# Square passes timed by the attention's row maxima, and three PSUM banks that are handed out oldest first

## The chip, the cores and the metric

One core of one Trainium2 chip runs the whole program in one launch. The metric is the device time of that launch in microseconds (us), lower being better. TensorE (PE) multiplies, VectorE (DVE), ScalarE (ACT) and GpSimd (POOL) do the rest, and SyncE (SP) issues nearly all transfers. Each engine works through its own queue in order; an instruction that must wait for another engine holds up everything behind it on its own queue. PSUM, into which TensorE writes, has eight banks here, each 128 partitions by 512 float32.

## The reference

For 8 batches: banded causal attention (8 heads, 576 positions, head size 64, a window of 128 and a slope per head), the real part of a two-dimensional Fourier transform added to its output, a layer norm, and a feed-forward network of width 2048 with a residual.

```python
scores = scale * np.matmul(q, k.transpose(0, 1, 3, 2))
...
scores = np.where(mask, scores + bias[None], -1000000000.0)
scores = scores - np.max(scores, axis=-1, keepdims=True)
attn = np.exp(scores)
attn = attn / (np.sum(attn, axis=-1, keepdims=True) + 1e-09)
return np.matmul(attn, v).astype(np.float32)
...
X = np.fft.fft(x, axis=1)
X = np.fft.fft(X, axis=2)
u = x + np.real(X)
un = (u - mu) / np.sqrt(var + 1e-06)
ch = np.maximum(un @ w_ch1, 0.0) @ w_ch2
return (u + ch).astype(np.float32)
```

## The kernel before

**Work.** The 8 batches have 4 pairs of heads each, so there are 32 pairs p, with b = p // 4. A pair's attention is three groups of scores (`scores`, L387): TensorE writes them into the PSUM tiles `sp0` and `sp1`, VectorE adds the bias and takes each row's maximum in one instruction per tile (L415, into the small tile `nb`), and ScalarE takes the exponential with `nb` as its bias (shown at L169, the helper `after`). From batch 2 on (NF = 2) products run on fp16 pairs: ScalarE rounds to the high half (L428), VectorE makes the low half (shown at L169), SP transposes both by DMA (L437, `pt<-P`), and `values` (L453) multiplies with v into `pv`; `weigh` (L479) divides by the row sums into X (L491). Batches 0 and 1 work in float32 and transpose on TensorE instead (`turn`, L439); there `warm` (L321) adds products that nobody reads, a number of them behind each turn.

When a batch's heads are done, `fourier` (L522) folds X on VectorE, multiplies it by tables on TensorE (`rows`, `middle`, `cols`) and adds the result to X; `norm` (L695) normalizes and sends it through DMA transposes to `uT`. The feed-forward `ffn` (L737) multiplies `uT` by the first weights in steps (L752: 24 matmuls of 256 columns fill one PSUM tile `fp`), ScalarE takes the ReLU (L757), VectorE makes the low half `hbuf` (L169), and the second product (L767: 48 matmuls of 512 columns fill one `fp`) is added to X by VectorE (`X<-fp`, or `ut<-fp` for the rest rows that two batches share) and stored.

**Scale passes.** For each batch from 2 on, `batch_scales` (L258) needs a bound of the sums of squares of q, k and v: 15 chunks are fetched by DMA into slots of `wall` (L273) and squared by ScalarE with a running sum into `mx` (L278, the "Square"). From batch 3 on (75 chunks) each fetch is held back: POOL first copies one element into the slot (L272), from the piece of X that `weigh` was last recorded to write (`last[-1]`), and the DMA has to follow that copy. `top` (L282) and `total` (L152) finish a pass.

**Order.** Every step is put on a heap with a due time in units of about 5 us, and the kernel's main loop records them in order of these times (`put`, `after`); the constants at the top are due times and lengths of steps. A scheduler of the language then orders each engine's queue by its own model of time and by the data dependencies that it sees, so a small copy that depends on other work also moves what follows it.

**Banks.** Four of the eight hold `sp0` and `sp1`, one `pv`. Two more form the pool `ps_f`, used in turn for `fp` (feed-forward; in batch 0 some of the transform). The last, `ps_d` (tile `pd`), holds the sums of the scale passes and the transform's products from batch 1 on, one after another.

Of the kernel before, what the change touches and what calls it, by code (L numbers as in the profile page):

```python
# [22 lines left out]
NF = 2  # L23
# [21 lines left out]
E0 = 18.423  # L45
W1A, N0 = 1.058, 20
WL = (-2.569, 0.042)
PL, VL = 8.86, 2.996
FL, SA, SD, SB, SE = 1.9, 16.181, 0.696, 24.163, 1.152
DFT = 29.394  # L50
START = 48.432
PACE, T1 = (0.447, 0.427), 13.742
SPIN, GAP = 5, 0.73
SLOW = 1.609
W2A, W2D, W2B, W2E = 13.895, 0.631, 21.285, 0.429
W1D, W1B, W1E = 0.379, 11.116, 0.508
F0 = 6.021
SW = 184
SPIN1 = 1


def begin_of(p):
    return 6 * PACE[0] * p if p < 4 else T1 + 6 * (p - 4)


def transform_of(b):
    return T1 + 24 * (b - 1) + DFT if b else PACE[0] * DFT

# [14 lines left out]
def attn_fft_ffn_kernel(  # L83
# [24 lines left out]
    ps_f, ps_s = pool("ps_f", 2, space=PSUM), pool("ps_s", 2, space=PSUM)  # L108
    ps_v, ps_d = pool("ps_v", 1, space=PSUM), pool("ps_d", 1, space=PSUM)
# [42 lines left out]
    def total(m):  # L152
        sums = ps_d.tile([128, 512], F32, name="pd")[:, 0:m.shape[1]]
        T.matmul(sums, misc[:, 7:8].broadcast_to([128, 128]), m, start=True, stop=True)
        return sums
# [20 lines left out]
    last = []  # L176

    def weights(wi, t0, dt, t1, dt1):
# [26 lines left out]
        def gram(c):  # L205
            if c == 0:
                box["gram"] = ps_f.tile([128, 512], F32, name="fp")[:, 0:128]
# [50 lines left out]
    def batch_scales(b, t0, dt):  # L258
# [6 lines left out]
        def fetch(x, fl, o, n):  # L265
# [5 lines left out]
            if b > NF:  # L271
                G.tensor_copy(box[x][1][0:1, 0:1], last[-1])  # L272
            nc.sync.dma_start(out=box[x][1], in_=fl[:, o:o + n])  # L273

        def part(x, i, c):
            slot, t = box.pop(x)
            held.discard(slot)
            A.activation(t, t, AF.Square, accum_out=box["mx"][:, i, c:c + 1])  # L278

        def top():  # L280
            m1 = small.tile([128, 3], F32, name="m1")
            V.tensor_reduce(m1, box["mx"], AX.X, ALU.max)  # L282
            box["sums"] = total(m1)

        def scale():
            r = small.tile([128, 3], F32, name="r")
            root_inv(r, box["sums"])
            sc = small.tile([128, 8], F32, name="sc", bufs=3)
# [98 lines left out]
    def scores(p, i):  # L387
# [19 lines left out]
        for e in range(2):  # L407
# [3 lines left out]
            for ti in grp:  # L411
# [4 lines left out]
                                       mul, 3.0e38, ALU.add, ALU.min, nb[:m, ti:ti + 1])  # L416
                after(0.25, A.activation, pt[:m, 0:n], pt[:m, 0:n], AF.Exp, bias=nb[:m, ti:ti + 1], scale=-1.0)
# [21 lines left out]
    def turn(p, i, e):  # L439
# [11 lines left out]
        after(GAP, warm, upper, SPIN if p < 4 else SPIN1)  # L451
# [27 lines left out]
    def weigh(p, e, pv):  # L479
# [13 lines left out]
        last.append(Xs[b][0:1, 0, h * D:h * D + 1])  # L493
# [441 lines left out]
```

## Time and profile before

| | us |
|---|---|
| median of 3 runs (1077.57 to 1080.9) | 1079.5 |
| the profiled execution, its own time | 1086.17 |
| its span (first to last instruction) | 1083.9 |
| TensorE busy in the span | 1039.0 |
| VectorE, ScalarE, POOL busy | 703.2, 583.0, 48.0 |
| granted clock, mean | 0.984 |

The 2.3 us between the span and the execution's own time lie outside the instructions. A row of a wait view names who waited, whose end released it, the total, how often, and the longest. In the timeline a bracket gives the engine's idle time before the row and what ended it. TensorE's matmuls overlap in their pipeline, so a row of one matmul is longer than the distance to the next.

### The profile page before, as it was taken

What the parts mean: (1) busy time and instruction counts of PE and PEld (TensorE: products, weight loads), DVE (VectorE), ACT (ScalarE), POOL (GpSimd) and SP (SyncE); (2) the same over time, 40 slices, a digit from 0 to 9 for tenths busy, and PEclk for the clock granted to TensorE, in tenths of its full rate; (3) what the DMA queues carried; (4) which work ended last, traced back from release to release, by engine and by line L of the source; (5) the groups of instructions that cost most, each with busy time, mean ns of one, the idle gap of its engine ahead of it and who ended that gap; (6) DMA issues with size and microseconds to landing.
All of it is one profiled execution on the core that took longest, in us unless ns stands there. A gap on an engine that the chain in (4) does not pass through costs nothing.

```text
span 1083.9 us, 23935 instructions
## 1 busy us (share of the span) xinstructions
PE 1039.0 (96%) x9208; PEld 726.4 (67%) x9208; DVE 703.2 (65%) x2073; ACT 583.0 (54%) x1388; POOL 48.0 (4%) x136
## 2 busy tenths in 40 slices
PE   8998889899899999999899999999999999999998
PEld 5876776675667667675657667584757676757655
DVE  4889789687674868687674858678784836252111
ACT  6886987558444567567554556556544522241000
POOL 0000001000000000001100000001000000000000
PEclk8998989999999999999999999999999999999999
DMA  9961466727542364527643364537522330030000
GB/s 365 346 218 56 123 147 158 151 54 187 136 101 75 97 147 123 147 51 152 170 109 74 96 146 119 143 54 134 110 60 34 53 69 11 10 60 11 20 10 21
DMA packets 191506, 117.81 MB, mean 109 GB/s; under 512 B 154400, under 2 KB 164128, under 8 KB 191392
## 3 DMA queue, kind: packets, MB, share of 16 engines
q1 hardware_dynamic: 190816, 114.84, 42.4%
q8 instruction: 72, 1.18, 0.5%
q10 hardware_dynamic: 576, 1.45, 0.3%
q14 instruction: 42, 0.34, 0.1%
HBM read 70.63 MB, written 9.44 MB: 74 GB/s over the span
## 4 chain that ended last, share of the span: by engine, by line
PE 61%; DVE 16%; DMA 9%; ACT 7%; issue 3%; SPq 2%; POOL 1%; ACTq 0%; DVEq 0%; POOLq 0%
PE fp L752 25%; PE fp L767 22%; PE sp L403 4%; DMA wall<-v_dram 4%; DVE P L415 2%; DMA wall<-q_dram 2%; ACT wall L278 2%; PE pd L602 2%; PE pv L468 2%; DVE P L169 1%; PE pd L636 1%; DVE hbuf L169 1%; DMA pt<-P 1%; ACT P L169 1%; PE sp L446 1%
## 5 line engine op out<-in xcount | busy, mean ns | idle before, releaser
L767 PE MATMUL fp<-wall,hbuf 128*128 128x512 f16 x1728 | 391.2, 379 | 0.0
L752 PEld LDWEIGHTS <-wall 128*128 128x128 f16 x3840 | 338.5, 99 | 70.4 <-issue 25.2
L752 PE MATMUL fp<-uT,wall 128*128 128x256 f16 x3072 | 365.4, 275 | 20.2 <-DVE hbuf L169 11.9
L767 PEld LDWEIGHTS <-hbuf 128*128 128x128 f16 x1728 | 162.8, 98 | 184.9 <-issue 3.5
L757 ACT ACTIVATE hbuf<-fp 128x512 f16<-128x512 f32 x144 | 84.8, 589 | 202.0 <-PE fp L752 201.9
L169 ACT ACTIVATE P<-P,nb 128x256 f32<-128x256 f32 x320 | 141.9, 477 | 60.8 <-DVE nb L415 60.5
L169 DVE SCALAR_TENSOR_TENSOR hbuf<-fp,hbuf 128x512 f16<-128x512 f32 x144 | 98.8, 686 | 99.3 <-ACT hbuf L757 98.4
L169 DVE SCALAR_TENSOR_TENSOR P<-P 128x256 f16<-128x256 f32 x240 | 87.4, 391 | 40.4 <-ACT P L428 38.9
L415 DVE CUSTOM_DVE_ANT_0 P<-sp,rg,nsl 128x256 f32<-128x256 f32 x240 | 97.5, 449 | 13.7 <-PE sp L403 12.0
L278 ACT ACTIVATE wall<-wall 128x512 f32<-128x512 f32 (+2 forms) x90 | 54.4, 605 | 91.3 <-DMA wall<-k_dram 33.5
L403 PE MATMUL sp<-kk,qq 64*128 64x256 f16 (+5 forms) x880 | 95.0, 287 | 1.4 <-ACT pt L449 0.7
L428 ACT ACTIVATE P<-P 128x256 f16<-128x256 f32 x240 | 84.1, 382 | 2.4 <-DMA pt<-P 1.7
L473 PE MATMUL pv<-vhs,pt 128*128 128x65 f16 x432 | 56.0, 195 | 1.2 <-DMA pt<-P 1.1
L474 PE MATMUL pv<-vl,pt 128*128 128x64 f16 x432 | 55.9, 193 | 0.0
L169 DVE SCALAR_TENSOR_TENSOR X<-fp,misc,X 128x512 f32<-128x512 f32 x32 | 23.8, 744 | 48.4 <-PE fp L767 48.3
L475 PE MATMUL pv<-vhs,pt 128*128 128x65 f16 x432 | 55.1, 194 | 0.0
L403 PEld LDWEIGHTS <-qq 64*128 64x128 f16 (+1 forms) x720 | 32.4, 99 | 24.6 <-issue 18.8
L473 PEld LDWEIGHTS <-pt 128*128 128x128 f16 x432 | 41.0, 98 | 9.6 <-issue 1.3
L752 PE MATMUL fp<-wall,wall 128*128 128x128 f16 x768 | 46.2, 219 | 0.0
L474 PEld LDWEIGHTS <-pt 128*128 128x128 f16 x432 | 40.7, 99 | 6.1
L468 PEld LDWEIGHTS pv<-vr,pt 128*128 128x128 f32 x288 | 37.6, 199 | 6.1 <-PE pv L323 3.3
L272 POOL COPY wall<-X 1x1 f32<-1x1 f32 x75 | 26.2, 377 | 343.9 <-DVE X L491 265.0
(159 smaller groups left out, 1205.9 us busy)
## 6 DMA issues: line engine op xcount, KB each, us to landing
qr<-q_dram SPq DMA_DIRECT2D x32, 304.0 KB, 3.2
hbuf<-w_dram SPq DMA_DIRECT2D x16, 512.0 KB, 7.7
out_dram<-X SPq DMA_DIRECT2D x32, 256.0 KB, 2.2
wall<-v_dram SPq DMA_DIRECT2D x30, 256.0 KB, 3.5
vr<-v_dram SPq DMA_DIRECT2D x24, 320.0 KB, 4.1
kr<-k_dram SPq DMA_DIRECT2D x24, 289.0 KB, 3.8
wall<-q_dram SPq DMA_DIRECT2D x24, 256.0 KB, 3.0
wall<-k_dram SPq DMA_DIRECT2D x24, 256.0 KB, 3.1
```

The costliest lines, as they stand in the source:

```text
L169: put(now[0] + dt, lambda: f(*a, **kw))
L278: A.activation(t, t, AF.Square, accum_out=box["mx"][:, i, c:c + 1])
L403: T.matmul(sp[e][:m, col:col + n], qq[h, c0:c0 + m], keys(kk[h], ti), start=(x == 0), stop=(x == len(prods) - 1))
L415: V.tensor_tensor_reduce(pt[:m, 0:n], sp[e][:m, col:col + n], tab[:m, pc:pc + n], mul, 3.0e38, ALU.add, ALU.min, nb[:m, ti:ti + 1])
L428: A.activation(hi, P32, AF.Copy, scale=2.0 ** 14)
L468: T.matmul(pv[:, ti], pt[:, col:col + 128], ops[p][2][:, e, vc], start=first, stop=last)
L473: T.matmul(pv[:, ti], ph, vh[:, e, vc], start=first, stop=False)
L474: T.matmul(pv[:, ti, 0:D], ph, vl[:, e, vc], start=False, stop=False)
L475: T.matmul(pv[:, ti], pl, vh[:, e, vc], start=False, stop=last)
L752: T.matmul(fp[:, i * n:(i + 1) * n], w1_ap(e, c, f0 + i), uT[:, j, c, 0:n], start=(c == 0 and p == 0), stop=(c == 3 and p == 2))
L757: A.activation(ht[:, 0], fp, AF.Relu)
L767: T.matmul(op, hh[f][:, a, i * 128:(i + 1) * 128], w2_ap(e, f), start=(f == 0 and p == 0), stop=(f == 15 and p == 2))
```

## The change

Three things are edited. First, the POOL copy ahead of a fetch reads `mark[-1]`, the row maximum last recorded, where it read the last piece of X; and a new POOL instruction ahead of each of these 75 Squares writes zero (a row maximum minus itself) into the cell of `mx` that the Square then fills, so that the Square follows the row maximum last recorded at its own due time. Second, three banks are now one set: up to the start of the feed-forward of batch 1 they are given out as before, and from then on `take` gives the one that was given back the longest ago (`give`, recorded with the last reader). Third, due times change: among them the distance of the pairs of batch 1 (0.911 of a unit's six), the start of the feed-forwards, the length of a transform (1.386 for 1.609), the lead of a fetch (2.073 for 1.9), and six `warm` products in place of five behind each turn of pair 1.

```diff
-FL, SA, SD, SB, SE = 1.9, 16.181, 0.696, 24.163, 1.152
+FL, SA, SD, SB, SE = 2.073, 16.745, 0.696, 24.163, 1.152
-SLOW = 1.609
-W2A, W2D, W2B, W2E = 13.895, 0.631, 21.285, 0.429
+SLOW = 1.386
+W2A, W2D, W2B, W2E = 16.635, 0.564, 21.18, 0.402
...
-    return 6 * PACE[0] * p if p < 4 else T1 + 6 * (p - 4)
+    return 6 * PACE[0] * p if p < 4 else T1 + 6 * PQ * (p - 4) if p < 8 else T1 + T2 + 6 * (p - 4)
...
-    ps_f, ps_s = pool("ps_f", 2, space=PSUM), pool("ps_s", 2, space=PSUM)
-    ps_v, ps_d = pool("ps_v", 1, space=PSUM), pool("ps_d", 1, space=PSUM)
+    ps_s, ps_v = pool("ps_s", 2, space=PSUM), pool("ps_v", 1, space=PSUM)
+    banks = [pool(f"ps_b{i}", 1, space=PSUM) for i in range(3)]
+    stamp, taken, late, turn2, ticks = [0, 0, 0], {}, [], cycle((0, 1)), count(1)
+
+    def take(key, name):
+        assert key not in taken
+        if late:
+            i = min((i for i in range(3) if i not in taken.values()), key=lambda i: stamp[i])
+        else:
+            i = next(turn2) if name == "fp" else 2
+        taken[key] = i
+        return banks[i].tile([128, 512], F32, name=name, tag="bank")
+
+    def give(key):
+        stamp[taken.pop(key)] = next(ticks)
...
             if b > NF:
-                G.tensor_copy(box[x][1][0:1, 0:1], last[-1])
+                G.tensor_copy(box[x][1][0:1, 0:1], mark[-1])
             nc.sync.dma_start(out=box[x][1], in_=fl[:, o:o + n])
...
             held.discard(slot)
+            if b > NF:
+                G.tensor_tensor(box["mx"][0:1, i, c:c + 1], mark[-1], mark[-1], ALU.subtract)
             A.activation(t, t, AF.Square, accum_out=box["mx"][:, i, c:c + 1])
...
+                mark.append(nb[0:1, ti:ti + 1])
                 after(0.25, A.activation, pt[:m, 0:n], pt[:m, 0:n], AF.Exp, bias=nb[:m, ti:ti + 1], scale=-1.0)
...
-        last.append(Xs[b][0:1, 0, h * D:h * D + 1])
...
+    def lower(key, ht, fp):
+        V.scalar_tensor_tensor(ht[:, 1], fp, 0.0, ht[:, 0], ALU.max, ALU.subtract)
+        give(key)
+
+    def joined(key, t, op):
+        V.scalar_tensor_tensor(t, op, wone, t, ALU.mult, ALU.add)
+        give(key)
+
     def ffn(b):
+        if b:
+            late.append(b)
...
-                fp = ps_f.tile([128, 512], F32, name="fp")
+                key = ("first", b, slot, f0)
+                fp = take(key, "fp")
```

How the order moves is shown at the fifth chunk of q of batch 4 (384 wide). On POOL, where `X` is the output of batch 3 and `nb` a group's row maxima, the fetches of batch 4's first six chunks stood before like this (the fifth chunk's copy is in the fourth row):

```order
L272 COPY wall0_109<-X_2498 1x1 x2
L272 COPY wall1_110<-X_2498 1x1
L642 MEMSET ab_2771 128x2
L272 COPY wall0_109<-X_2498 1x1 x2
L272 COPY wall1_110<-X_2498 1x1
L263 MEMSET mx_5464 128x15
```

and after the change, from the second chunk on, like this (the fifth chunk's copy is the first that reads `nb_3836`, and its Square's own instruction is in the last row):

```order
L732 TENSOR_TENSOR rstd_3032<-rstd_3032,misc_97 128x2
L288 COPY wall0_112<-nb_3600 1x1
L288 COPY wall1_113<-nb_3600 1x1
L295 TENSOR_TENSOR mx_3560<-nb_3600 1x1
L732 TENSOR_TENSOR rstd_3130<-rstd_3130,misc_97 128x1
L288 COPY wall0_112<-nb_3701 1x1
L295 TENSOR_TENSOR mx_3560<-nb_3701 1x1
L288 COPY wall0_112<-nb_3836 1x1
L295 TENSOR_TENSOR mx_3560<-nb_3836 1x1 x2
L288 COPY wall1_113<-nb_3836 1x1
L288 COPY wall0_112<-nb_3988 1x1
L295 TENSOR_TENSOR mx_3560<-nb_3988 1x1 x2
```

The fetches no longer stand in bunches behind one piece of X, but one or two to a group of row maxima. On ACT, the same chunk's Square (`mx`, 384 wide) stood before among these (L169 with `nb` is an exponential, L757 a ReLU):

```order
L169 ACTIVATE P_3999<-P_3999,nb_3998 128x256
L757 ACTIVATE hbuf_108<-fp_3794 128x512
L378 ACTIVATE qq_4245<-qr_4084,nsl_3346 128x608
L428 ACTIVATE P_4033<-P_3999 128x256
L378 ACTIVATE kk_4325<-kr_4085,sc_3340 128x578
L169 ACTIVATE P_4002<-P_4002,nb_4001 128x256
L428 ACTIVATE P_4035<-P_4002 128x256
L278 ACTIVATE wall0_109,mx_3542<-wall0_109 128x384
L757 ACTIVATE hbuf_108<-fp_3857 128x512
L278 ACTIVATE wall1_110,mx_3542<-wall1_110 128x512
L278 ACTIVATE wall0_109,mx_3542<-wall0_109 128x512
L757 ACTIVATE hbuf_108<-fp_3915 128x512
```

and after the change among these:

```order
L448 ACTIVATE P_3866<-P_3834 96x256
L183 ACTIVATE P_3839<-P_3839,nb_3836 96x256
L296 ACTIVATE wall1_113,mx_3560<-wall1_113 128x512
L448 ACTIVATE P_3868<-P_3837 128x256
L296 ACTIVATE wall0_112,mx_3560<-wall0_112 128x512
L448 ACTIVATE P_3870<-P_3839 96x256
L788 ACTIVATE hbuf_111<-fp_3873 128x512
L788 ACTIVATE hbuf_111<-fp_3921 128x512
L397 ACTIVATE qq_4260<-qr_4073,nsl_3356 128x608
L183 ACTIVATE P_3986<-P_3986,nb_3985 128x256
L183 ACTIVATE P_3989<-P_3989,nb_3988 128x256
L296 ACTIVATE wall0_112,mx_3560<-wall0_112 128x384
```

Where two exponentials of the group ahead (`nb_3998`, `nb_4001`) stood between older work and the Square, there are now the end of the group whose maximum let the fetch go (`nb_3836`) and all of the next one (`nb_3985`, `nb_3988`). On DVE, the piece of X that released the fetch (L491, `X_2498`) stood before between the row maxima `nb_3998` and `nb_4001`, the latter being what the last exponential ahead of the Square reads:

```order
L415 ISA P_3999,nb_3998<-sp0_3990,rg_3349,nsl_3346 128x256
L415 ISA nb_3998 128x1
L169 SCALAR_TENSOR_TENSOR P_3882<-P_3851,P_3882 128x256
L169 SCALAR_TENSOR_TENSOR hbuf_108<-fp_3763,hbuf_108 128x512
L169 SCALAR_TENSOR_TENSOR P_3884<-P_3853,P_3884 96x256
L489 TENSOR_SCALAR ri_3814<-pv_3656,sc_1997 128x5
L490 RECIPROCAL ri_3814<-ri_3814 128x5
L491 TENSOR_TENSOR X_2498<-pv_3656,ri_3814 128x5x64
L415 ISA P_4002,nb_4001<-sp1_3991,rg_3349,nsl_3346 128x256
L415 ISA nb_4001 128x1
L169 SCALAR_TENSOR_TENSOR hbuf_108<-fp_3794,hbuf_108 128x512
L169 SCALAR_TENSOR_TENSOR qq_4245<-qr_4084,nsl_3346,qq_4245 128x608
```

After the change the fetch goes with `nb_3836` (first row), and the last exponential ahead of the Square reads `nb_3988`:

```order
L434 ISA P_3839,nb_3836<-sp1_3818,rg_3359,nsl_3356 96x256
L434 ISA nb_3836 96x1
L183 SCALAR_TENSOR_TENSOR P_3864<-P_3832,P_3864 128x256
L758 SCALAR_TENSOR_TENSOR hbuf_111<-fp_3804,hbuf_111 128x512
L183 SCALAR_TENSOR_TENSOR P_3866<-P_3834,P_3866 96x256
L183 SCALAR_TENSOR_TENSOR P_3868<-P_3837,P_3868 128x256
L183 SCALAR_TENSOR_TENSOR P_3870<-P_3839,P_3870 96x256
L758 SCALAR_TENSOR_TENSOR hbuf_111<-fp_3873,hbuf_111 128x512
L758 SCALAR_TENSOR_TENSOR hbuf_111<-fp_3921,hbuf_111 128x512
L434 ISA P_3986,nb_3985<-sp0_3977,rg_3359,nsl_3356 128x256
L434 ISA nb_3985 128x1
L434 ISA P_3989,nb_3988<-sp1_3978,rg_3359,nsl_3356 128x256
```

Before, one row maximum lay between the release of the fetch and the last exponential ahead of the Square; now seven rows of other work and a whole next group do.

## Rows read from the trace of the kernel before

**Rows 1.** The page's first part, busy time, share of the span and number of instructions of each engine.

```profile
PE 1039.0 (96%) x9208; PEld 726.4 (67%) x9208; DVE 703.2 (65%) x2073; ACT 583.0 (54%) x1388; POOL 48.0 (4%) x136
```

**Rows 2.** The windows view of five stretches: length, busy time and number of instructions of TensorE, its weight loads, VectorE, ScalarE and POOL, then the granted clock, the DMA engines' share and GB/s. Scale passes run in the first four stretches, none in the last.

```profile
66.00:165.00 99.00, 88.28 (x676) 70.53 (x674) 82.69 (x257) 83.04 (x185) 2.68 (x12) 0.90 0.47 127
165.00:284.00 119.00, 109.23 (x1006) 74.39 (x1005) 90.99 (x277) 78.18 (x197) 9.71 (x24) 0.99 0.62 141
284.00:529.00 245.00, 235.95 (x2235) 162.15 (x2234) 170.88 (x516) 142.21 (x354) 15.01 (x43) 1.00 0.48 115
529.00:773.00 244.00, 237.58 (x2241) 163.01 (x2239) 175.50 (x525) 139.54 (x344) 15.23 (x34) 0.99 0.48 112
773.00:895.00 122.00, 122.00 (x1176) 83.97 (x1175) 77.64 (x218) 52.50 (x126) 1.69 (x5) 1.00 0.32 60
```

**Rows 3.** The waits view of TensorE between 165 and 773 us: who waited for whom, total us, times, longest.

```profile
PE fp L752 <- DVE hbuf L169: 11.9, 10, 2.7
PE fp L752 <- DVE X L169: 4.3, 3, 2.3
PE fp L752 <- DVE ut L169: 3.5, 2, 2.5
PE pd L602 <- DVE zl L610: 3.5, 3, 2.1
PE pv L473 <- DMA pt<-P: 1.1, 1, 1.1
PE pd L602 <- ACT fh L575: 0.8, 1, 0.8
```

**Rows 4.** The waits view of ScalarE over the whole span, its waits for the fetches of the scale passes.

```profile
ACT wall L278 <- DMA wall<-k_dram: 33.5, 17, 4.6
ACT wall L278 <- DMA wall<-q_dram: 29.0, 14, 5.1
ACT wall L278 <- DMA wall<-v_dram: 28.5, 13, 5.2
```

**Rows 5.** The timeline of 272.9 to 281 us, the rows of several engines in order of time: start, length, engine, line, what, in brackets the idle time before it and what ended it.

```profile
272.97 0.49 DVE L491 TENSOR_TENSOR X<-pv,ri 128x320 f32<-128x320 f32 x1
273.59 0.41 POOL L272 COPY wall<-X 1x1 f32<-1x1 f32 x3 [18.05 <-ACT P L428]
274.99 0.52 SPq L273 DMA_DIRECT2D wall<-q_dram  x1
277.96 0.19 PE L475 MATMUL pv<-vhs,pt 128*128 128x65 f16 x1
277.99 0.19 PE L473 MATMUL pv<-vhs,pt 128*128 128x65 f16 x1
278.98 0.52 ACT L278 ACTIVATE wall<-wall 128x384 f32<-128x384 f32 x1 [3.88 <-DMA wall<-q_dram]
279.51 0.58 ACT L757 ACTIVATE hbuf<-fp 128x512 f16<-128x512 f32 x1
280.11 0.69 DVE L169 SCALAR_TENSOR_TENSOR hbuf<-fp,hbuf 128x512 f16<-128x512 f32 x1 [3.49 <-ACT hbuf L757]
280.86 0.38 PE L752 MATMUL fp<-uT,wall 128*128 128x256 f16 x2 [2.67 <-DVE hbuf L169]
```

**Rows 6.** The source view of L272, POOL's copies ahead of the fetches: duration in ns as least, median and longest, first and last start; below it what they waited for (us, times).

```profile
L272 POOL COPY wall<-X x75: 173/174/2801, 140.0 to 693.9; 1x1 f32<-1x1 f32 x75
  DVE X L491: 265.0, 24
```

**Rows 7.** The source view of L273, the fetches: time from issue to landing, in us.

```profile
DMA to landing us min/median/max: 2.1/3.2/6.1
```

**Rows 8.** The timeline around 757 us, rows of VectorE and TensorE.

```profile
756.61 0.06 DVE L544 MEMSET pm<- 96x4 f32 x1 [3.59 <-DMA uT<-un]
758.77 0.74 DVE L169 SCALAR_TENSOR_TENSOR X<-fp,misc,X 128x512 f32<-128x512 f32 x1
759.57 0.60 PE L752 MATMUL fp<-uT,wall 128*128 128x256 f16 x4 [2.31 <-DVE X L169]
```

**Rows 9.** The windows view of two stretches of 4 us, columns as in rows 2.

```profile
281.00:285.00 4.00, 4.00 (x27) 2.98 (x26) 0.69 (x1) 0.79 (x3) 0.00 (x0) 0.57 0.69 146
646.00:650.00 4.00, 3.93 (x21) 2.90 (x21) 1.24 (x4) 0.57 (x2) 0.00 (x0) 0.57 0.68 169
```

**Rows 10.** The chain of waits in order of time, two of its last pieces: start, length, what.

```profile
954.99 20.72 PE fp L767 x96
975.71 20.96 PE fp L752 x192
```

**Rows 11.** The page's fifth part, groups of instructions: busy us, mean ns of one, idle before. A ReLU and its low half, an exponential.

```profile
L757 ACT ACTIVATE hbuf<-fp 128x512 f16<-128x512 f32 x144 | 84.8, 589 | 202.0 <-PE fp L752 201.9
L169 DVE SCALAR_TENSOR_TENSOR hbuf<-fp,hbuf 128x512 f16<-128x512 f32 x144 | 98.8, 686 | 99.3 <-ACT hbuf L757 98.4
L169 ACT ACTIVATE P<-P,nb 128x256 f32<-128x256 f32 x320 | 141.9, 477 | 60.8 <-DVE nb L415 60.5
```

**Rows 12.** The waits view of TensorE from 0 to 165 us, its two longest entries.

```profile
PE pv L323 <- ACT pt L449: 3.1, 2, 2.2
PE pv L323 <- DVE X L491: 2.8, 1, 2.8
```

**Rows 13.** The groups of TensorE by line, the products that nobody reads.

```profile
L323 PE MATMUL pv<-pt 128*128 128x184 bf16 x144 | 20.9, 253 | 5.9 <-ACT pt L449 3.1 <-DVE X L491 2.8
```

More of the change, by code (lines that the diff above doesn't have):

```diff
@@ L150, in view, with total @@
         return bass.AP(tensor=t.tensor, offset=t.offset + off, ap=[t.ap[0]] + [list(d) for d in dims])
-    def total(m):
-        sums = ps_d.tile([128, 512], F32, name="pd")[:, 0:m.shape[1]]
+    def total(key, m):
+        sums = take(key, "pd")[:, 0:m.shape[1]]
         T.matmul(sums, misc[:, 7:8].broadcast_to([128, 128]), m, start=True, stop=True)
@@ L175, in attn_fft_ffn_kernel @@
     weighed, valued = [0] * B, [0] * 4 * B
-    last = []
+    mark = []
     def weights(wi, t0, dt, t1, dt1):
@@ L206, in gram @@
             if c == 0:
-                box["gram"] = ps_f.tile([128, 512], F32, name="fp")[:, 0:128]
+                box["gram"] = take(("gram", wi), "fp")[:, 0:128]
             upper = words(c)[1].bitcast(BF16).rearrange("p (x e) -> p x e", e=2)[:, :, 1]
@@ L282, in top @@
             V.tensor_reduce(m1, box["mx"], AX.X, ALU.max)
-            box["sums"] = total(m1)
+            box["sums"] = total(("scale", b), m1)
         def scale():
@@ L287, in scale @@
             root_inv(r, box["sums"])
+            give(("scale", b))
             sc = small.tile([128, 8], F32, name="sc", bufs=3)
@@ L450, in turn @@
         upper = pt.bitcast(BF16).rearrange("p (x e) -> p x e", e=2)[:, :, 1]
-        after(GAP, warm, upper, SPIN if p < 4 else SPIN1)
+        after(GAP, warm, upper, SPL[p])
     def values(p, i, e):
@@ L512, in attn_fft_ffn_kernel, with bank @@
     uts, uTs = {}, {}
-    spare = cycle((ps_f, ps_d, ps_f))
-    def bank(b):
-        if b == 0:
-            p = next(spare)
-            return p.tile([128, 512], F32, name="fp" if p is ps_f else "pd")
-        return ps_d.tile([128, 512], F32, name="pd")
+    spare = cycle(("fp", "pd", "fp"))
+    def bank(key):
+        return take(key, next(spare) if key[1] == 0 else "pd")
     def fourier(b, t0):
@@ L594, in rows @@
         def rows(g):
-            zp = st["zp", g] = bank(b)
+            zp = st["zp", g] = bank(("rows", b, g))
             o = 0 if g < 2 else 2
@@ L610, in rows_lo @@
             V.scalar_tensor_tensor(zl, st["zp", g][:, :NS], 2.0 ** -19, st["zh", g], ALU.mult, ALU.subtract)
+            give(("rows", b, g))
         def middle():
-            gps = st["gps"] = bank(b)
+            gps = st["gps"] = bank(("middle", b))
             for j, (j0, mj) in enumerate(SCH):
@@ L625, in middle_out @@
                 A.activation(gt[:mj, 1, j:j + 1], gt[:mj, 0, j:j + 1], AF.Copy, scale=-1.0)
+            give(("middle", b))
         gw = (129, 128, 128, 127)
@@ L631, in cols @@
             j0, m = SCH[j]
-            mp = st["mp", j] = bank(b)
+            mp = st["mp", j] = bank(("cols", b, j))
             for g in range(4):
@@ L665, in cols_add @@
                 V.tensor_tensor(ut[p0 + 64:p0 + 96], X2[64:96], ds[64:96, 0:512], ALU.add)
-        f = (SLOW if b > 1 else 0.9) if b else PACE[1]
+        f = (SLOW if b > 1 else F1) if b else PACE[1]
         put(t0, begin)
@@ L757, in ffn @@
                 A.activation(ht[:, 0], fp, AF.Relu)
-                after(0.2, V.scalar_tensor_tensor, ht[:, 1], fp, 0.0, ht[:, 0], ALU.max, ALU.subtract)
+                after(0.2, lower, key, ht, fp)
                 for i in range(per):
@@ L762, in ffn @@
             for i, t in enumerate(tiles):
-                op = ps_f.tile([128, 512], F32, name="fp")
+                key = ("second", b, slot, i)
+                op = take(key, "fp")
                 for f in range(16):
@@ L770, in ffn @@
                         yield
-                after(0.15, V.scalar_tensor_tensor, t, op, wone, t, ALU.mult, ALU.add)
+                after(0.15, joined, key, t, op)
                 after(0.4, nc.sync.dma_start, out=ov[slot + i], in_=t)
@@ L777, in attn_fft_ffn_kernel @@
         b, j = divmod(p, 4)
-        t, f = begin_of(p), 1 if b else PACE[0]
+        t, f = begin_of(p), 1 if b > 1 else (PACE[0], PQ)[b]
         lead = t - (7 if b else PL) * f if p else -3.2
```

29 lines of the change are left out of this document (17 added, 12 removed).

## Prediction

> **What bounds the kernel now.** I read the page's busy shares first, then the stretches, then who waits for whom, and last the timeline at one wait. TensorE is busy 1039.0 of 1083.9 us [rows 1], so at most some 45 us of its idle time can be won, and the rest of the time is matmuls that the change leaves as they are. The stretches say where that idle time lies [rows 2]: 10.7 us in 66 to 165, 9.8 in 165 to 284, 9.1 in 284 to 529, 6.4 in 529 to 773, and nothing in 773 to 895. The last stretch still has attention, a transform and feed-forward side by side, but no scale pass. That is the best control in this trace: without the passes, two banks for the feed-forward and one for the transform let TensorE run without a gap.
>
> Between 165 and 773 us, 25.1 us of waits have names [rows 3]. In nearly all, TensorE wants a bank and VectorE has not read it yet. VectorE is not the cause: ScalarE waits 91.0 us in all, 44 times, at a Square whose chunk has not landed [rows 4], and the ReLUs behind it wait too. At 273 us the whole chain can be seen [rows 5]: weigh writes X at 272.97, POOL copies three times in a bunch at 273.59, the fetch is issued at 274.99, the Square starts at 278.98 after 3.88 us of idle, the ReLU follows at 279.51, VectorE reads the bank at 280.11, and TensorE, idle for 2.67 us, goes on at 280.86. X written to Square started took 6.0 us. In the order before, only one row maximum stands on VectorE between that X and the last exponential ahead of this Square.
>
> **The Squares' waits.** I counted over both orders how many VectorE instructions lie between the one that releases a fetch (or what POOL and SP must pass before it) and the one that the last ScalarE instruction ahead of its Square needs. Before, the median of the 75 held-back chunks is 3, and for 32 it is zero or less; after the change it is 23, and none is zero or less. A VectorE record lasts 703.2 / 2073 = 0.34 us, and VectorE is busy 65% of the time, so 23 are some 8 to 12 us, an estimate, against the 6.0 us that the chain needs (of which 3.2 us median landing [rows 7]). Some 12 instructions, 4 us of work or 6 with idle, are then the border; counting to 15 to be safe, 70 of 75 lie under it before and 15 of 73 after (for two, other waits hide the fetch). So I keep 20% of what the waits cost and let 80% go.
>
> What they cost TensorE: the waits for `hbuf` (11.9), `ut` (3.5), `zl` (3.5) and `fh` (0.8) [rows 3], 19.7 us. 80% of it is 15.8. Bounds: 0, if something else is late next, and 19.7.
>
> **The banks.** A bank of the feed-forward's first product holds 24 matmuls of 20.96 / 192 = 0.109 us, 2.6 us; one of the second holds 48 of 20.72 / 96 = 0.216 us, 10.4 us [rows 10]. Emptying a bank takes a ReLU of 0.59 and a low half of 0.69 us [rows 11]. With two banks, the second `fp` of a batch takes the bank of the last second product, one block of 2.6 us after that ended. At 757 us VectorE stood 3.59 us for a DMA transpose that was still reading its buffer, so the addition to X came at 758.77 and TensorE waited 2.31 us [rows 8]. Oldest first, that block takes a bank that was freed before or during that second product; in the order, 11 to 15 us of matmuls lie between its last use and this one for batches 2 to 5. The three `X` waits (4.3 us) should go by the same 80%: 3.4. Where the transform runs, it now shares the three banks with the feed-forward. Its own reuse comes no sooner (3.1 us of matmuls at the tightest for `rows` before, and after once the set is shared), but the single tile of `middle` and the one after it have only 2.7 to 3 us where they had up to 5.4. One feed-forward block of batch 1 has 1.6 us behind `middle`; I charge 1 us for these. The first transform from the old single bank, batch 1's, stays as tight as it was.
>
> **What each wait costs on top.** A matmul's record is 0.19 us where the next could start 0.03 us later [rows 5], so a wait of the list is some 0.16 us longer than printed: 80% of 20 waits, 16 x 0.16 = 2.6. And behind two of the longest the granted clock is 0.57, from 281 to 285 and from 646 to 650 us [rows 9], that is the lower of its two levels, 1.2 GHz, for most of it and 2.4 GHz for the rest: 2 x 4 x 0.43 = 3.4 us. With the waits gone I let this go too.
>
> **What is added.** 75 POOL instructions of one element, 0.17 us median each if they last as the copies do [rows 6]. They wait for the same row maximum as an exponential that ScalarE has to run ahead of the Square anyway, 0.48 us [rows 11], which covers 0.17; uncovered, they would be 75 x 0.17 = 12.8 us of ScalarE, of which TensorE felt 19.7 / 91.0 = 0.22, so 2.8 us. The row maxima's buffer is used again only some 50 VectorE instructions later. Here a page speaks against the change: the Trainium skill, "SBUF — State Buffer", section "Who interferes with whom", says that a VectorE instruction with two SBUF inputs and a GpSimd instruction that reads SBUF exclude each other for a whole instruction. The longest copy, 2.8 us against a median of 0.17, would fit that, the median does not. By the row's median the sum has nothing for this; by the rule at its worst it would be turned into a loss of some 15 us, which is rival 4.
>
> **Due times and the start.** Six more dummy products are 0.25 us at most each by their record, 20.9 / 144 = 0.15 by busy time [rows 13]: 6 x 0.15 = 0.9. Up to 165 us the order moves everywhere, with waits of 3.1 and 2.8 us at the dummy products [rows 12]; there ScalarE and VectorE are busy 83 of 99 us beside TensorE's 88 [rows 2], so nothing is free. The banks are as before there. In the order, batch 0's feed-forward is some 3 us further when batch 2's scores begin, and other waits are tighter. I take 0, with 6 us either way.
>
> **Sum.** 15.8 + 3.4 + 2.6 + 3.4 - 1 - 0.9 = 23.3. The profiled execution took 1086.2 us, 2.3 of it outside its span, so 1062.9 there; it ran 6.7 us above the median, and I take that to be the same part of a later run. From the median, 1079.5 - 23.3 = 1056.2.
>
> **Rivals.** (1) Something else is late next. VectorE is busy 76% of 165 to 284 [rows 2], and its queue of low halves can be the limit when ScalarE no longer is; half of the sum comes, 1068. Against it stands the last stretch without a gap, with VectorE at 64%. (2) All of it goes, with no wait left as in the last stretch: 25.1 + 3.2 + 3.4 = 31.7, less 1.9, and some 3 us in the start: 1047. (3) The start loses 6 to 8 us by the new due times, and the rest comes as summed: 1063. (4) Slower: the new POOL instruction heads the way of each Square. If VectorE's work holds it up, it lasts up to the 2.8 us of the longest copy [rows 6]; less the 0.48 us that an exponential covers, 75 x 2.3 = 173 us of ScalarE, times 0.22 is 38 us more, against 23 won: 1094. It decides from about 1.9 us each on ((23.3 / 0.22) / 75 = 1.4, plus 0.48); the 75 copies show a median of 0.17, so it is unlikely. (5) The pacing does not bind, because landings stretch as far as releases move ahead: the time stays, 1079.
>
> **How the numbers follow.** Forecast 0.5, rival 1 0.17, rival 2 0.16, rival 3 0.10, rival 4 0.04, rival 5 0.03. The likeliest time is 1056. The range 1045 to 1068 takes in the forecast with its start either way, rival 2's time, rival 3 and the upper half of rival 1. About 0.3% (3.2 us) is what a measurement can tell from no change; faster than that: 0.92, within: 0.04, slower: 0.04.
>
> **What would show it.** Right: ScalarE's waits for the fetches fall from 91.0 to 30 us or less; TensorE's waits for `hbuf`, `ut` and `zl` after 165 us fall under 6 us; no lower clock after 165 us; POOL's copies no longer come in threes. Wrong: Squares that now wait for POOL, row maxima that wait for it, or more idle time of TensorE in 66 to 165 us than 10.7 us.

## The result, and the profile after

| | median us | against before, 95% interval |
|---|---|---|
| before, run beside it | 1080.2 (4 runs) | |
| after | 1052.77 (4 runs, 1049.97 to 1052.84) | 0.9736 [0.9701, 0.9772] |

The ratio is estimated from the single runs of both kernels; the quotient of the two medians is 0.9746. The forecast was 1056 in 1045 to 1068. The profiled execution took 1052.83 us and spans 1051.0, 32.9 less than before; the profiled execution of before lay 6.7 us above the median of its runs, that of after on its median. First the page's busy shares of the kernel after:

```profile
PE 1027.8 (98%) x9214; PEld 721.6 (69%) x9214; DVE 701.1 (67%) x2073; ACT 582.2 (55%) x1388; POOL 77.4 (7%) x211
```

Against [rows 1], TensorE's idle time fell from 44.9 to 23.2 us (21.7), and its busy time by 11.2, with six more instructions: together the 32.9. The windows view of the kernel after, columns as in [rows 2], says where:

```profile
66.00:165.00 99.00, 91.29 (x703) 73.04 (x700) 80.92 (x249) 82.33 (x179) 3.84 (x12) 0.86 0.40 110
165.00:284.00 119.00, 111.67 (x1052) 75.97 (x1051) 96.08 (x297) 82.65 (x208) 18.23 (x46) 1.00 0.71 153
284.00:529.00 245.00, 244.65 (x2318) 167.21 (x2316) 185.19 (x555) 148.65 (x372) 27.14 (x77) 1.00 0.55 122
529.00:773.00 244.00, 243.78 (x2329) 167.39 (x2328) 182.62 (x553) 142.58 (x354) 22.06 (x54) 1.00 0.52 114
773.00:895.00 122.00, 122.00 (x1157) 86.07 (x1154) 69.38 (x185) 45.89 (x107) 1.70 (x5) 1.00 0.20 42
```

From 284 to 773 us TensorE is idle 0.6 us (0.35 + 0.22) where it was 15.5 [rows 2]; the stretches with scale passes now look like the last one, without. Before 284 us it keeps 7.7 and 7.3 of the 10.7 and 9.8. The granted clock is 1.00 in every stretch from 165 us on, but 0.86 for 0.90 in the first. TensorE's waits from 165 to 773 us in the kernel after (L783 and L799 are the two products, L758 the low half, L619 the transform's products, L493 values):

```profile
PE pv L493 <- DMA pt<-P: 2.5, 2, 1.6
PE pv L493 <- DVE X L511: 2.2, 2, 1.6
PE pd L619 <- DVE zl L627: 1.2, 1, 1.2
PE pd L619 <- ACT fh L592: 0.8, 1, 0.8
PE fp L799 <- DVE hbuf L758: 0.7, 1, 0.7
PE fp L783 <- DVE hbuf L758: 0.4, 2, 0.2
```

The waits for `hbuf`, 11.9 in [rows 3], are 1.1; those for `ut` and for X at the first product are gone. ScalarE's waits at a Square (now L296), over the whole span of the kernel after:

```profile
ACT wall L296 <- POOL mx L295: 6.6, 8, 2.7
ACT wall L296 <- DMA wall<-q_dram: 6.1, 3, 3.7
ACT wall L296 <- DMA wall<-k_dram: 4.1, 2, 3.2
ACT wall L296 <- DMA wall<-v_dram: 2.4, 2, 1.9
```

For the fetches it waits 12.6 us, 7 times, where it was 91.0 and 44 times [rows 4]. Landing takes about as long as before (2.1, 2.9 and 6.2 us as least, median and longest, against [rows 7]), so the fetches start earlier ahead of their Squares and hardly run faster.

### The profile page after: what moved, and what is told of

Its sections match the earlier page's. It is cut to its first block, busy times and chain, and to the rows that moved or that the text cites. A ratio compares the mean times of both kernels' runs of the same rounds, so it can differ in the third digit from the quotient of the medians.

```text
span 1051.0 us, 24075 instructions
## 1 busy us (share of the span) xinstructions
PE 1027.8 (98%) x9214; PEld 721.6 (69%) x9214; DVE 701.1 (67%) x2073; ACT 582.2 (55%) x1388; POOL 77.4 (7%) x211
## 3 DMA queue, kind: packets, MB, share of 16 engines
q1 hardware_dynamic: 190816, 114.84, 44.9%
## 4 chain that ended last, share of the span: by engine, by line
PE 83%; DVE 8%; DMA 3%; ACT 3%; issue 2%; POOL 0%; SPq 0%; ACTq 0%; DVEq 0%; POOLq 0%
PE fp L799 32%; PE fp L783 31%; PE sp L422 6%; PE pv L488 3%; PE pd L619 3%; DMA pt<-P 2%; DVE P L434 1%; PE sp L466 1%; PE pv L342 1%; PE pv L493 1%; PE pd L655 1%; PE pv L495 1%; PE pv L494 1%; DVE hbuf L758 1%; PE fp L225 1%
## 5 line engine op out<-in xcount | busy, mean ns | idle before, releaser
L799 PE MATMUL fp<-wall,hbuf 128*128 128x512 f16 x1728 | 393.2, 379 | 0.7 <-DVE hbuf L758 0.7
L783 PEld LDWEIGHTS <-wall 128*128 128x128 f16 x3840 | 337.6, 98 | 43.1 <-issue 4.3
L783 PE MATMUL fp<-uT,wall 128*128 128x256 f16 x3072 | 358.3, 273 | 0.4 <-DVE hbuf L758 0.4
L799 PEld LDWEIGHTS <-hbuf 128*128 128x128 f16 x1728 | 162.9, 98 | 183.2 <-issue 3.7
L758 DVE SCALAR_TENSOR_TENSOR hbuf<-fp,hbuf 128x512 f16<-128x512 f32 x144 | 98.4, 685 | 87.9 <-ACT hbuf L788 87.2
L448 ACT ACTIVATE P<-P 128x256 f16<-128x256 f32 x240 | 86.7, 382 | 14.0 <-DMA pt<-P 11.5
L422 PE MATMUL sp<-kk,qq 64*128 64x256 f16 (+4 forms) x880 | 89.1, 289 | 1.5 <-DVE m L173 1.0
L296 ACT ACTIVATE wall<-wall 128x512 f32<-128x512 f32 (+2 forms) x90 | 54.1, 602 | 22.2 <-POOL mx L295 6.6
L288 POOL COPY wall<-nb 1x1 f32<-1x1 f32 x75 | 34.2, 459 | 339.0 <-DVE nb L434 225.1
L493 PE MATMUL pv<-vhs,pt 128*128 128x65 f16 x432 | 54.1, 195 | 4.7 <-DMA pt<-P 2.5
L495 PE MATMUL pv<-vhs,pt 128*128 128x65 f16 x432 | 53.7, 193 | 0.0
L493 PEld LDWEIGHTS <-pt 128*128 128x128 f16 x432 | 41.0, 98 | 14.2 <-issue 4.1
L422 PEld LDWEIGHTS <-qq 64*128 64x128 f16 (+1 forms) x720 | 29.9, 99 | 24.1 <-issue 18.8
L783 PE MATMUL fp<-wall,wall 128*128 128x128 f16 x768 | 45.0, 219 | 0.0
```

The lines of the kernel that those rows point to most:

```text
L422: T.matmul(sp[e][:m, col:col + n], qq[h, c0:c0 + m], keys(kk[h], ti), start=(x == 0), stop=(x == len(prods) - 1))
L448: A.activation(hi, P32, AF.Copy, scale=2.0 ** 14)
L493: T.matmul(pv[:, ti], ph, vh[:, e, vc], start=first, stop=False)
L495: T.matmul(pv[:, ti], pl, vh[:, e, vc], start=False, stop=last)
L758: V.scalar_tensor_tensor(ht[:, 1], fp, 0.0, ht[:, 0], ALU.max, ALU.subtract)
L783: T.matmul(fp[:, i * n:(i + 1) * n], w1_ap(e, c, f0 + i), uT[:, j, c, 0:n], start=(c == 0 and p == 0), stop=(c == 3 and p == 2))
```

## The experiments

The change has three edits that can be undone apart: P, the pacing at both ends; B, the set of three banks; T, the due times. All eight combinations have a time:

| parts | kernel | median us | against before, 95% interval | TensorE idle, 284 to 773 us | ScalarE's waits for fetches |
|---|---|---|---|---|---|
| none | before | 1079.5 | 1 | 15.5 | 91.0 |
| none | all_off | 1085.76 | 1.0051 [1.0025, 1.0077] | 12.5 | 87.4 |
| P | pace_alone | 1074.14 | 0.9955 [0.9928, 0.9982] | 9.6 | 10.0 |
| B | banks_alone | 1089.03 | 1.0077 [1.0053, 1.0101] | 20.6 | 105.3 |
| T | times_alone | 1103.08 | 1.0203 [1.0149, 1.0256] | 31.2 | 74.7 |
| B T | no_pacing | 1071.97 | 0.9921 [0.9892, 0.9950] | 9.1 | 87.0 |
| P T | no_banks | 1091.47 | 1.0108 [1.0082, 1.0135] | 21.4 | 11.1 |
| P B | old_due_times | 1058.01 | 0.9813 [0.9797, 0.9828] | 2.6 | 23.9 |
| P B T | after | 1052.77 | 0.9736 [0.9701, 0.9772] | 0.6 | 12.6 |

Idle is a stretch's length less TensorE's busy time, the third and fourth stretches of the windows view together. The medians stem from three groups of runs, each with its own runs of before (1079.88, 1078.61, 1081.84), so the ratios are what to compare.

In the expectations P, B and D are the theories that the pacing, the banks or the due times by themselves make the gain (P is the prediction's); Q is that each edit needs another; S is that the tie at the Square is what counts, F the tie at the fetch.

### One edit at a time

**pace_alone** puts the pacing into the kernel before:

```diff
-                G.tensor_copy(box[x][1][0:1, 0:1], last[-1])
+                G.tensor_copy(box[x][1][0:1, 0:1], mark[-1])
...
+            if b > NF:
+                G.tensor_tensor(box["mx"][0:1, i, c:c + 1], mark[-1], mark[-1], ALU.subtract)
```

> The kernel before with only the first edit: fetches and Squares timed by row maxima at both ends, old banks, old due times. Theory P (ScalarE late behind its Squares is the cause of TensorE's waits): about 1060 us (1055 to 1066), ScalarE's waits for the fetches fall from 91 us to 35 or less, TensorE's waits for hbuf, ut and zl after 165 us to 6 or less. Rival B (too few banks is the cause): about 1075, ScalarE's waits fall as well but TensorE's stay above 12 us. Rival D (the new due times bring it): about 1078.

Measured: 0.9955, 5.7 us under its runs of before, where P wanted some 20. TensorE's waits from 165 to 773 us in this kernel (L754 the first product, L476 values):

```profile
PE pv L476 <- DMA pt<-P: 8.7, 4, 3.2
PE fp L754 <- DVE X L169: 4.1, 2, 2.2
PE fp L754 <- DVE hbuf L169: 1.6, 1, 1.6
PE pd L604 <- ACT fh L577: 1.4, 1, 1.4
PE pd L604 <- DVE zl L612: 0.8, 1, 0.8
```

The step on the Squares did what was summed: ScalarE's waits fell from 91.0 to 10.0, and TensorE's for `hbuf`, `ut`, `zl` and `fh` from 19.7 to 3.8, so 15.9 went where 15.8 was forecast. Then the next comes late: the DMA transposes of P, 1.1 us in [rows 3], take 8.7, and the X waits stay at 4.1. The timeline of the longest, around 525 us, rows of ScalarE, SP and TensorE:

```profile
524.57 0.63 ACT L280 ACTIVATE wall<-wall 128x512 f32<-128x512 f32 x1 [1.41 <-DMA wall<-k_dram]
525.19 0.70 ACT L431 ACTIVATE P<-P 128x256 f16<-128x256 f32 x2
526.11 2.50 SPq L440 DMA_TRANSPOSE pt<-P  x2
526.82 0.83 PE L405 MATMUL sp<-kk,qq 64*128 64x256 f16 x12
530.85 0.24 PE L476 MATMUL pv<-vhs,pt 128*128 128x65 f16 x1 [3.20 <-DMA pt<-P]
```

ScalarE waits 1.41 us at a Square and rounds P right behind it, then SP issues two transposes. TensorE's last work ahead of their landing is the scores of a next group, done at 527.65, and then it stands 3.20 us. The Square's wait is less than half of that; why the order leaves TensorE so little to do there was not tried. Of the granted clock this kernel still has stretches at the lower level after 165 us: 3.4 us at 273.9 and at 287.5, 6.8 us at 529.9, behind that wait. That is rival 1, something else late next, in this kernel.

**banks_alone** is the kernel after with the fetches released by the last piece of X, without the Square's POOL instruction, and with the due times of before:

```diff
-                G.tensor_copy(box[x][1][0:1, 0:1], mark[-1])
+                G.tensor_copy(box[x][1][0:1, 0:1], last[-1])
...
-            if b > NF:
-                G.tensor_tensor(box["mx"][0:1, i, c:c + 1], mark[-1], mark[-1], ALU.subtract)
```

> The changed kernel with the fetches released by the last piece of X again, no instruction ahead of the Squares, and the old due times: only the set of three banks is new. Theory P: ScalarE still waits some 90 us for its fetches; a third bank gives TensorE one block of 2.6 us more, so it hides part: about 1070 (1064 to 1077). Rival B: about 1060, TensorE's waits nearly gone although ScalarE still waits 90 us. Rival D: about 1077.

Measured: 1.0077, above every expectation. ScalarE's waits at a Square in this kernel:

```profile
ACT wall L294 <- DMA wall<-q_dram: 46.2, 17, 7.5
ACT wall L294 <- DMA wall<-k_dram: 35.5, 18, 5.5
ACT wall L294 <- DMA wall<-v_dram: 23.6, 14, 4.0
```

A third bank does nothing for a ScalarE that stands 105.3 us for fetches: the X waits at the first product, which the oldest-first order was to remove, are 9.7 us (4.3 before), with `hbuf` at 7.1 and `fh` at 6.1.

**times_alone** puts the new due times into the kernel before, such as:

```diff
-SLOW = 1.609
+SLOW = 1.386
...
-FL, SA, SD, SB, SE = 1.9, 16.181, 0.696, 24.163, 1.152
+FL, SA, SD, SB, SE = 2.073, 16.745, 0.696, 24.163, 1.152
```

> The kernel before with only the new due times, old release of the fetches, old banks. Theory P and rival B: 1080 within 5 us, since the fetches are still released by X and the banks are the old ones. Rival D: about 1065.

Measured: 1.0203, the slowest of all and above every expectation. `hbuf` waits are 17.9 us, pt 10.4, `fh` 4.5, and TensorE's idle time from 284 to 773 us doubles to 31.2. The clock is at its lower level for 58.4 us of the span (34.6 in before). So 0 for the due times was not right: by themselves they cost 2%.

**all_off** is the code of after with all three undone (the diffs of banks_alone and times_alone, and `late` never filled). It computes what before does, with as many instructions on TensorE, VectorE, ScalarE and POOL (9208, 2073, 1388 and 136); the two differ in the order.

> The changed kernel's code with all three edits switched off: old release, nothing ahead of the Squares, banks given out as before throughout, old due times. It issues the same instructions as the kernel before, in an order that differs in places only. Every theory: within 5 us of 1080; what it differs by is what the scheduler's order alone is worth, a bound below which the single edits' differences say nothing.

Measured: 1.0051 [1.0025, 1.0077]. So an order that differs by accident is worth half a per cent here, by this one sample. TensorE is idle 3.0 us less from 284 to 773 us than in before, but its clock is at the lower level for 52.7 us of the span, where it was 34.6. The ratio of pace_alone is no further from 1 than that (0.45%). That of banks_alone is (0.77%), but its code is that of all_off, and 1.0077 / 1.0051 is 0.3%. Neither edit alone has an effect that can be told from an accident of the order.

### One edit taken away

**no_pacing** is after with the diff of banks_alone, its due times kept.

> The changed kernel without its first edit: new banks and due times, fetches released by the last piece of X, nothing ahead of the Squares. Theory P: about 1068 (most of the gain lost). Rival B: about 1056. Rival D: about 1060.

Measured: 0.9921; of the expectations theory P's comes nearest, with more than half of the gain lost. ScalarE waits 87.0 us for fetches as it did before, and still TensorE is idle 9.1 us in place of 15.5: with B and T together a good part of ScalarE's lateness no longer reaches TensorE.

**no_banks** keeps two banks and one:

```diff
-            late.append(b)
+            pass
```

> The changed kernel with the banks given out as before throughout (two in turn for the feed-forward, one for the transform and the sums); pacing and due times new. Theory Q (after the first four runs: pacing takes away ScalarE's waits, but what is late next is a bank, so each edit needs another one): 1068 to 1080, ScalarE's waits for its fetches under 25 us, TensorE waiting for hbuf, X and zl again, more than 10 us of it after 165 us. Theory P (pacing is the cause, the rest little): about 1058.

Measured: 1.0108; from here to after the set is worth 3.7%. ScalarE waits only 11.1 us for fetches, so that cure is whole, and the kernel is slower than before all the same. TensorE's waits from 165 to 773 us in this kernel:

```profile
PE pv L493 <- DMA pt<-P: 13.9, 6, 5.3
PE pd L619 <- ACT fh L592: 6.6, 3, 5.0
PE fp L783 <- DVE hbuf L758: 3.1, 4, 2.2
PE fp L799 <- DVE hbuf L758: 2.9, 3, 1.5
PE pd L619 <- DVE zl L627: 1.7, 1, 1.7
```

The transposes' wait is back at 13.9 us (2.5 in after). Theory Q's figures missed here: the time lies above its 1068 to 1080, and the waits that it named (`hbuf`, X, `zl`) come to 7.7 us, not more than 10; what is late are the transposes and `fh`. Against after, TensorE is idle 20.8 us more from 284 to 773 us, and its clock is at the lower level for 65.3 us of the span in place of 30.7, at half the speed at most another 17 us. So a good part of what the set is worth comes through the clock, behind the waits.

**old_due_times** is after with the due times of before, the diff of times_alone the other way round.

> The changed kernel with the old due times; pacing and the set of three banks new. Theory Q: pacing and banks fit each other, so about 1062 (1056 to 1068), and the due times bring the last 5 to 10 us. Rival R (banks given out by the time of release must fit the due times, as banks alone lost 8 us): about 1072, with waits of the transform for ScalarE's or VectorE's folds.

Measured: 0.9813, inside theory Q's range, so P and B make most of it and T the last 0.8%. TensorE's waits from 165 to 773 us in this kernel:

```profile
PE pd L619 <- ACT fh L592: 3.5, 2, 3.0
PE pd L619 <- DVE fl L604: 2.4, 3, 1.4
PE pv L493 <- DVE X L511: 0.6, 1, 0.6
PE fp L783 <- DVE hbuf L758: 0.5, 1, 0.5
```

No wait for pt has a row (8.7 us with P alone), and `hbuf` is at 0.5. The transform does wait for its folds, 5.9 us, as rival R has it, but the time is not R's. Theories P, B and D fall as stated. Q stands in its main point, that each edit needs another, though not in what it expected to be late.

### Which end of the pacing

**fetch_end_only** is after without the POOL instruction ahead of the Square; **square_end_only** is after with the fetches still released by X:

```diff
-            if b > NF:
-                G.tensor_tensor(box["mx"][0:1, i, c:c + 1], mark[-1], mark[-1], ALU.subtract)
```

```diff
-                G.tensor_copy(box[x][1][0:1, 0:1], mark[-1])
+                G.tensor_copy(box[x][1][0:1, 0:1], last[-1])
```

> The changed kernel without POOL's instruction ahead of each Square: only the fetch is released by a row maximum. If the earlier release alone counts: within 3 us of 1052, and POOL's 75 instructions less. If the second end matters (it keeps the scheduler from putting a Square ahead of the row maxima of its due time): 1058 to 1066, with ScalarE waiting for its fetches 40 us or more.

> The changed kernel with its fetches released by the last piece of X again, and POOL's instruction ahead of each Square kept. Theory S (the order keeps a Square away from its fetch only if the Square itself is tied to a row maximum; by the count over the order the median distance is 26 VectorE instructions here, 23 in the changed kernel, 0 with the fetch end alone): 1050 to 1057, ScalarE's waits for its fetches under 35 us. Rival F (both ends are needed): 1058 to 1066, waits over 50 us.

Measured: 0.9858 [0.9833, 0.9883] and 0.9772 [0.9741, 0.9803]. ScalarE's waits at a Square, first with the fetch's end alone:

```profile
ACT wall L294 <- DMA wall<-q_dram: 34.1, 20, 5.5
ACT wall L294 <- DMA wall<-v_dram: 33.7, 19, 3.3
ACT wall L294 <- DMA wall<-k_dram: 19.7, 13, 3.5
```

and with the Square's end alone:

```profile
ACT wall L296 <- DMA wall<-v_dram: 7.1, 5, 2.7
ACT wall L296 <- DMA wall<-q_dram: 6.5, 4, 3.7
ACT wall L296 <- DMA wall<-k_dram: 3.3, 1, 3.3
```

With the fetch's end alone, ScalarE waits 87.5 us for fetches, as before; with the Square's alone 16.9. The prediction's count says why. VectorE instructions between a fetch's release and its Square, median of the chunks: 3 before, 0 with the fetch's end alone, 26 with the Square's alone, 23 with both. When a fetch is released earlier and nothing holds its Square, the scheduler moves the Square up as well. The tie that delays the consumer makes the distance. What the earlier release adds to it can't be told: the count is no larger with both ends, and the intervals of 0.9772 and 0.9736 overlap. Nor do ScalarE's waits alone set the time: the fetch's end alone takes the kernel from 0.9921 (no_pacing) to 0.9858 with the same 87 us of them, little more than an accident of the order is worth.

**pool_twice** has one more POOL instruction for each of the 75 Squares:

```diff
             if b > NF:
+                G.memset(box["mx"][:, i, c:c + 1], 0.0)
                 G.tensor_tensor(box["mx"][0:1, i, c:c + 1], mark[-1], mark[-1], ALU.subtract)
```

> The changed kernel with one more POOL instruction ahead of each Square, a memset of the cells of mx that it fills (128 by 1), so that POOL's part of the way is doubled. If the pacing instruction is hidden behind the exponential of its row maximum, as the prediction costs it: within 3 us of 1052. If it lies on ScalarE's way: 75 times some 0.1 to 0.3 us of ScalarE, of which TensorE feels a part: 1055 to 1060.

Measured: 0.9736 [0.9716, 0.9755], as after (median 1049.96). It tells less than was meant: the source view has the added instructions at 98 ns median from 150.0 to 451.2 us, while those ahead of the Squares start up to 681.3, so the scheduler put many of them long before their Squares. 75 more instructions on POOL cost nothing that this run can tell; one more on the Square's own way was not tried. What the present one costs is read directly: 6.6 us of ScalarE, above.

### The start

After has TensorE longer at the lower clock level in the start, 20.5 us from 85.8 on (10.2 from 86.7 before). **more_dummies** tries to fill that place with products that nobody reads; **set_from_batch0** hands out the set from the first feed-forward on:

```diff
-SPL = (5, 6, 5, 5, 1, 1, 1, 1)
+SPL = (5, 6, 5, 5, 4, 4, 1, 1)
```

```diff
-        if b:
-            late.append(b)
+        late.append(b)
```

> The changed kernel with four dummy products in place of one behind each turn of pairs 4 and 5, where its granted clock is at the lower level from 85.8 to 106.3 us. If that level there costs time: the lower stretch shrinks to 10 us or less and the time falls by 2 to 6 us, to 1047 to 1051. If the engines beside TensorE set the pace there (ScalarE and VectorE busy 82 of 99 us): the clock may rise, the time stays within 2 us of 1052 or grows by the 36 more products, 3 us.

> The changed kernel with the three banks given out oldest first from the first feed-forward (batch 0) on, in place of batch 1 on. If the waits left at 167 to 206 us (hbuf, zl, fh: 3 us) are those of two fixed banks and a single one: 1048 to 1052. If the transform of batch 1 loses its own bank to the feed-forward: 1053 to 1060.

Measured: 0.9824 [0.9793, 0.9854] and 0.9913 [0.9881, 0.9944], both slower than after, and each outside both of its expectations. The windows view of the first two stretches, more_dummies:

```profile
66.00:165.00 99.00, 90.68 (x650) 70.33 (x649) 77.80 (x249) 80.26 (x176) 2.68 (x12) 0.79 0.42 118
165.00:284.00 119.00, 113.31 (x1044) 78.10 (x1043) 92.66 (x283) 78.51 (x197) 17.36 (x42) 0.99 0.58 133
```

and of set_from_batch0:

```profile
66.00:165.00 99.00, 91.87 (x684) 73.78 (x685) 66.63 (x212) 68.15 (x159) 2.41 (x10) 0.84 0.37 99
165.00:284.00 119.00, 102.38 (x817) 62.37 (x817) 96.25 (x293) 82.06 (x191) 16.86 (x40) 0.89 0.59 137
```

The dummies don't lift the clock: the 20.5 us are there as in after, now from 87.6 on, and a second stretch of 20.5 follows at 128.6 (6.8 at 133.6 in after), with a wait of 2.9 us for uT inside it. In set_from_batch0 VectorE does only 66.6 us of work in the first stretch (80.9 in after) while TensorE works off feed-forward, and from 165 on TensorE is idle 16.6 us with a clock of 0.89, at scores whose queries and at products whose weights are being rounded. From 284 us on it is idle 0.4 us, as after. Why the set moves the order of the start so far was not settled.

## Why the prediction was right, and where its steps were not

- **The total** came 3.4 us under the forecast, well inside the range. The prediction's observables held: fetch waits of 12.6 us (30 or less), waits for `hbuf`, `ut` and `zl` of 2.3 (under 6), no lower clock after 165 us, TensorE idle 7.7 us from 66 to 165 (not over 10.7), and POOL's copies alone or in twos, where 14 threes stood back to back before. One of its signs of being wrong came too: Squares wait for POOL, 8 times, 6.6 us.
- **The Squares' waits** were sized right, 15.9 for 15.8 in pace_alone. The step that failed is what follows from it: that these microseconds are won without more. With two banks and one, half of them come back as waits for the transposes, the X waits stay, and the time falls by 5.7 us, no more than an accident of the order is worth.
- **The banks** were the mis-sized term: 3.4 us less 1, for the X waits alone. With the pacing in place the set is worth 1.4% with the due times of before (0.9955 to 0.9813, some 15 us) and 3.7% with the new ones (some 40). That it takes away the waits for the transposes is shown, from 8.7 to no row and from 13.9 to 2.5. How is argued from the order, and not shown: TensorE's work between the last use of a feed-forward bank and its next use is 3.8 us in the median with two banks and 5.6 or more with the set, so more feed-forward can stand ahead of the values. More room alone is not enough: banks_alone has it too, and is no faster.
- **The due times** were put at nothing. They are worth -0.8% with both others (0.9813 to 0.9736) and -1.5% on the set alone (1.0077 to 0.9921), and cost 2.0% alone and 1.5% on the pacing. So they pay with the set and cost without it. That a shorter transform (1.386 for 1.609) asks for denser work, which only the freer banks can carry, is an argument; which of the constants counts was not tried.
- **Clock and overhead** were 3.4 and 2.6; TensorE's busy time fell by 11.2. The stretches at the lower level last 34.6 us before and 30.7 after: up to 165 us there are 3.5 us more of them (27.2 and 30.7), and the 7.4 us behind that are gone. Half of the difference, 2.0 us, is the clock's part at most, so that term was too large. Of the other 9.2 us, the overhead of the waits explains some: TensorE's records leave 44 gaps before and 26 after, and 18 fewer at the prediction's 0.16 us are 2.9. What the remaining 6.3 us are isn't shown. The profiled execution of before lay 6.7 us above its median, so they may be no gain of the change at all.
- **The rivals.** Rival 1 is true of the pacing alone and not of the whole. Rival 2 comes nearest after 284 us, where 0.6 us is left, but not before. Rival 3: no idle time was lost in the start, only clock, 3.5 us more at the lower level, 1.8 us of time at most. Rival 4 has its mechanism in the trace (below) in 8 of 75 places and 6.6 us, not 173. Rival 5 falls: landing takes 2.9 us in the median, with the fetch's end alone too. There ScalarE's waits do stay (87.5 us), but because the Square moves up and not because landings stretch, and the time falls by 1.4% all the same.

The right time was in part luck. The largest term of the sum belongs to two edits together, and the due times, put at nothing, cost or gain with the banks; without the combinations, the pacing would have been credited with nearly all of it.

## What to carry to other kernels

To keep a transfer ahead of its use under a scheduler, tie the use, not only the release: an earlier release alone moved the consumer up with it and left the waits at 87.5 us. Count a cure for a late engine as won only with what is late next, and price buffers, pacing and timetable together: here each alone lay between -0.5 and +2.0%, and all three gave -2.6%. Run the unchanged work in the new code's order too (1.0051 here) before reading a half per cent from a single edit.

## What the runs showed of the hardware

**POOL under VectorE.** The 75 new instructions take 183 ns in the median and 3409 at most. The timeline of the longest in the kernel after, rows of POOL, VectorE and ScalarE:

```profile
174.81 3.75 POOL L295 TENSOR_TENSOR mx<-nb 1x1 f32<-1x1 f32 x2
175.26 0.35 DVE L570 TENSOR_TENSOR pm<-X 96x256 f32<-96x256 f32 x1
176.54 0.67 DVE L555 TENSOR_TENSOR fg<-X 128x512 f32<-128x512 f32 x1
177.14 0.67 DVE L556 TENSOR_TENSOR fg<-X 128x512 f32<-128x512 f32 x1
178.09 0.41 DVE L576 TENSOR_TENSOR abcd<-pm 96x256 f32<-96x256 f32 x1
178.25 0.52 ACT L296 ACTIVATE wall<-wall 128x384 f32<-128x384 f32 x1 [2.72 <-POOL mx L295]
```

VectorE runs back to back here, mostly sums and differences of two SBUF tiles (five of its rows are left out). POOL's row holds two instructions, and the first, of one element, lasts 3.41 us through all of it, so the Square waits 2.72 us. At 201.2 us another such instruction took 0.18 us in the middle of a low half (L758, 0.67 us), whose first input lies in PSUM. This agrees with the Trainium skill, "SBUF — State Buffer", section "Who interferes with whom", that a VectorE instruction with two SBUF inputs and a GpSimd instruction that reads SBUF keep each other out. The trace adds that a row of such instructions can hold POOL all through, and that it is rare here. One of the rows left out does not fit: VectorE begins the run with a memset, which reads nothing (174.85 us, 0.48 us), and POOL's instruction did not end during it. A POOL instruction that only writes is not held. These are the added memsets of pool_twice, by the source view (least, median and longest in ns):

```profile
L295 POOL MEMSET mx<- x75: 88/98/99, 150.0 to 451.2; 128x1 f32 x75
```

In the trace, 30 of the 75 lie wholly inside a low half of P on VectorE, which reads two SBUF tiles.

**The clock in the start.** The windows view of 85 to 107 us, first the kernel before, then the kernel after:

```profile
85.00:107.00 22.00, 19.70 (x142) 15.73 (x143) 19.81 (x55) 14.39 (x26) 0.10 (x1) 0.77 0.23 66
```

```profile
85.00:107.00 22.00, 20.12 (x78) 13.59 (x79) 19.19 (x55) 15.35 (x30) 0.10 (x1) 0.53 0.10 32
```

TensorE is busy as much in both, with 78 products in place of 142, and the granted clock is 0.77 and 0.53, that is half the stretch and nearly all of it at 1.2 GHz. Before the fall TensorE had waited 2.1 us for a turn in the kernel after (from 83.7 us), 0.7 and 0.9 us in the kernel before (from 84.8 and 86.5). The length of that wait does not settle how long the lower level lasts: in more_dummies it is 1.5 us, once, and the level lasts 20.5 us as in after. What goes with it over all kernels is where the last 64 products of `gram` stand (L211 before), which the due times and the new code's order move. In before most of them run without a gap inside the lower stretch, which ends at 96.9 us:

```profile
91.93 5.22 PE L211 MATMUL fp<-wall 128*128 128x128 bf16 x48
```

In pace_alone they stand there too, and both kernels have 10.2 us at the lower level. In the other twelve kernels they stand at 65 to 78 or at 118 to 125 us, and the lower level lasts 17.1 to 23.9 us; all_off, which does the work of before, is one of them. No run moved these products alone, so the cause stays open.
